# Fused LayerNorm, S5 scan and SwiGLU on one core: one row sum of the fast product made by an accumulating DMA, its seven products reordered

## The chip, the core and the metric

The kernel runs on one core of a Trainium2 chip. The metric is the device time of one execution in microseconds (us); shorter is better. Before the change the median of 7 runs is 204.39 us, from 203.69 to 205.23.

## The reference

The input x has 2048 rows (time steps) of 512 columns. With xn the layer-normalised x, the output is the sum of three things:

```python
xn = layernorm(x)
# S5: a complex diagonal recurrence over time, 512 states, then a projection
h[t] = Lam_bar * h[t-1] + xn[t] @ B_bar.T
ssm  = 2 * Re(h @ C.T) + xn * Dskip
# SwiGLU, inner width 1792
glu  = (silu(xn @ w1) * (xn @ w3)) @ w2
out  = x + ssm + glu
```

All inputs and the output are bf16.

## The kernel before

**Blocks and chunks.** The 2048 rows are worked in four blocks of 512 (b = 0 to 3), each of four chunks of 128 rows. For a block the kernel normalises and transposes xn, makes the gate tiles (`glu`, L519: two matmul groups for each of 14 inner tiles f; ScalarE evacuates both at L534 and L535, VectorE multiplies them at L543), makes the scan's input (`bu`, L425), and runs the scan on VectorE (`ssm_tasks`, L443: products with a cosine and sine table at L457 and L461, an add by an accumulating DMA at L468, scans at L478, products at L484 and L488, an accumulating DMA at L492). Gates and states end as 22 tiles of 128 inner columns, all in one fp16 buffer `act(b)`, of which there are two.

**The fast product.** The output of two chunks (a pair, n = 0 to 7, two for each block) is a product of a matrix A (256 rows by 22 inner tiles) with the stacked weights w2 and C (22 inner tiles by 512 columns). Split in halves both ways, it is a two-by-two product, and the kernel does it in Winograd's form with 7 products in place of 8. Each product (`mms`, L722) is 11 matmuls of 128x256. It needs sums of the blocks of A, and sums of the weights (`weight_sums`, made once). The sums of A are

- S1 = A21 + A22, S3 = A11 - A21, S2 = S1 - A11 (`row_sums`, L676), three VectorE instructions at L683 for each pair. S1 and S2 go to buffers of their own (`homes`), S3 is written over A21;
- S4 = A12 - S2 (L766), written over A12 inside `y_fast`.

**`y_fast(n)`, L708,** issues the seven products of a pair in this order: A11, S1, A12, S2, A22, S4, S3 (for the last pair S3 stands ahead of S4). They accumulate into four PSUM tiles named g, f, z and e; e is seeded by ScalarE at L705 (`seeds`) from the residual. Between the products ScalarE copies g to f and e to an fp32 strip `q[1]` (`copy`, L744), and VectorE adds PSUM tiles to the residual rows (`add`, L735). A finished chunk of 128 rows is stored to HBM by the SyncE queue at L738.

**What sets the order.** The order on each engine is written by the program and is fixed when it is built. Background VectorE work is kept in a list (`Filler`, L24); `fill` releases tasks from it as long as an account of VectorE's time stays within a lead of the account of TensorE's, and `flush(key)` releases all up to a key. Background ScalarE work is in a second list, `sins`; `steps()` in `y_fast` issues two of its entries at a place for block 0. There stand the LayerNorm statistics of blocks 2 and 3 (`ln_scalar_engine`, L262): for each of 4 chunks a sum (L269), then squares (L275), then the normalised row (L285), which ends with a DMA transpose on SyncE's queue (L242). Between these, GpSimd turns sums into a mean (L272) and squares into a reciprocal root (L278, L279, L280). GpSimd also issues the accumulating DMAs, in its program order.

**Around the pairs.** After the gates of block 1 come pairs 0 and 1 (block 0), then the gates of block 2, `bu(3)`, pairs 2 and 3 (block 1), the gates of block 3, and pairs 4 to 7.

Of the kernel before, what the change touches and what calls it, by code (L numbers as in the profile page):

```python
# [11 lines left out]
ALU = mybir.AluOpType  # L12
ACT = mybir.ActivationFunctionType

FP32 = DT.float32
BF16 = DT.bfloat16
FP16 = DT.float16
P = 128
# [45 lines left out]
def kernel(  # L64
# [454 lines left out]
    def glu(b):  # L519
        xnT = xnT_blk[b]  # L520
        pend = []

        def mms(ps, w, f, tsl):
            for dt in range(NDT):
                nc.tensor.matmul(out=ps[:, tsl], lhsT=w[:, dt, f * P:(f + 1) * P], rhs=xnT[:, dt, tsl],  # L525
                                 start=(dt == 0), stop=(dt == NDT - 1))

        pair = []

        def evac(f, g_ps, u_ps):  # L530
            if f % 2 == 0:
                pair[:] = [glup.tile([P, 2, TBLK], BF16, name="g16"), glup.tile([P, 2, TBLK], BF16, name="u16")]
            g16, u16 = pair
            nc.scalar.activation(out=g16[:, f % 2, :], in_=g_ps, func=ACT.Silu)  # L534
            nc.scalar.activation(out=u16[:, f % 2, :], in_=u_ps, func=ACT.Copy)  # L535
            if f % 2 == 1:
                pend.append((f, g16, u16))

        def gate():
            f, g16, u16 = pend.pop(0)  # L540
            bg.own(0.6, -0.5)
            k0, k1 = k_gate(f - 1), k_gate(f)
            nc.vector.tensor_tensor(out=act(b)[:, k0:k1 + 1:k1 - k0, :], in0=g16, in1=u16, op=ALU.mult)  # L543

        f0 = 0
        if b == 0:
            f0 = FIRST
            tiles = first_ps

            def quarter(cl, fs, parts=1):  # L550
                tsl = slice(cl * P, (cl + 1) * P)
                n = NDT // parts
                for side, w in ((0, w1_sb), (1, w3_sb)):
                    for i in range(0, NDT, n):
                        for f in fs:
                            for dt in range(i, i + n):
                                nc.tensor.matmul(out=tiles[2 * f + side][:, tsl], lhsT=w[:, dt, f * P:(f + 1) * P],  # L557
                                                 rhs=xnT[:, dt, tsl], start=(dt == 0), stop=(dt == NDT - 1))

            ln_stats(0, 0)  # L560
            ln_first_rstd(0)
            bulk_loads()
            ln_stats(0, 1)
            ln_first_rstd(1)
            ln_first_transpose(0, 2)
            keep_busy(4, P)
            ln_apply(0, 1)
            ln_first_transpose(1)
            ln_stats(0, 2)
            ln_first_rstd(2)  # L570
            ln_stats(0, 3)
            ln_first_rstd(3)
            ln_apply(0, 2)
            ln_apply(0, 3)
            quarter(0, (0, 1), 2)
            quarter(1, (0, 1))
            pps = params_transpose()
            params_dt(pps)
            params_turn()
            table_angles(0)  # L580
            table_angles(1)
            ln_first_transpose(2)
            quarter(0, (2,))
            ln_first_transpose(3)
            quarter(1, (2,))
            nc.scalar.activation(out=rho, in_=kr, func=ACT.Exp)
            nc.scalar.preload_act_table_set("silu_and_others")
            quarter(2, range(FIRST))
            for f in range(FIRST):
                quarter(3, (f,))  # L590
            evac(0, tiles[0], tiles[1])
            evac(1, tiles[2], tiles[3])
            evac(2, tiles[4], tiles[5])
            gate()
            bg.tensor(0.0)
            bg.fill()
        for f in range(f0, NFT):
            if f == AHEAD[b]:
                if b == 0:
                    ssm_tasks(0)  # L600
                bu(b)
            g_ps = ps_gu.tile([P, TBLK], FP32, name="gu_ps")
            mms(g_ps, w1_sb, f, slice(0, TBLK))
            u_ps = ps_gu.tile([P, TBLK], FP32, name="gu_ps")
            mms(u_ps, w3_sb, f, slice(0, TBLK))
            evac(f, g_ps, u_ps)
            if b in (1, NBLK - 1) and f == NFT - 3:
                seeds(0 if b == 1 else 4)
            if b == 0 and f == FIRST:
                sin_step((0, 0))  # L610
            elif b > 0 or f != MID - 1:
                sin_step()
            bg.tensor(1.72)
            bg.fill()
            if pend and f % 2 == 0:
                gate()
        return gate
# [29 lines left out]
    def weight_sums():  # L647

        def parts(kh, dsl):
            return w2_sb[:, kh * NFH:(kh + 1) * NFH, dsl], weight_state(kh, dsl)  # L650

        def own(i):
            return tw[:, i, 0:NFH, :], tw[:, i, NFH:NK, :]

        def in_place(v):
            return v[0].bitcast(FP16), v[1]

        b11, b12, b21, b22 = parts(0, D1), parts(0, D2), parts(1, D1), parts(1, D2)
        t1, (t2, t3, t4) = in_place(b12), (own(i) for i in range(3))
        def add(i, which):  # L660
            out, x, z = ((t1, b12, b11), (t2, b22, t1), (t3, b22, b12), (t4, b21, t2))[which]
            bg.add((1.1, 0.7)[i], lambda: nc.vector.tensor_tensor(
                out=out[i], in0=x[i], in1=z[i], op=ALU.subtract), "tw")

        return add

    def sum_homes():
        n = NK * P
        spare = tw[:, 3, :, :].rearrange("p k d -> p (k d)")
        xs = [x_blk[i].rearrange("p c d -> p (c d)") for i in range(2)]  # L670
        q = [v[:, n:n + 2 * DH].bitcast(FP32) for v in (*xs, bt.rearrange("p r t d -> p (r t d)"))]
        return [[v[:, 0:n] for v in xs], [spare[:, 0:n], spare[:, n:2 * n]]], q

    sums = {}
# [1 line left out]
    def row_sums(n, b, p):  # L676
# [1 line left out]
        r1, r2 = slice(2 * p * P, (2 * p + 1) * P), slice((2 * p + 1) * P, (2 * p + 2) * P)  # L678
        a11, a12 = a[:, 0:NK, r1], a[:, NK:2 * NK, r1]
        a21, a22 = a[:, 0:NK, r2], a[:, NK:2 * NK, r2]  # L680
        s1, s2 = (v.bitcast(FP16).rearrange("p (k t) -> p k t", t=P) for v in homes[n % 2])
        sums[n] = dict(a11=a11, a12=a12, a22=a22, s1=s1, s2=s2, s3=a21)
        return [(0.9, lambda out=out, x=x, z=z, op=op: nc.vector.tensor_tensor(out=out, in0=x, in1=z, op=op), ("sums", n))  # L683
                for out, x, z, op in ((s1, a21, a22, ALU.add), (a21, a11, a21, ALU.subtract),
                                      (s2, s1, a11, ALU.subtract))]

    seeded = {}

    def seeds(n):
        b, p = pairs[n]  # L690
# [17 lines left out]
    def y_fast(n, then=()):  # L708
# [26 lines left out]
            nc.vector.tensor_tensor(out=out, in0=x, in1=w, op=ALU.add)  # L735

        def store(cl, o, dsl=slice(0, D), eng=nc.sync):
            eng.dma_start(out=ov[:, b * CPB + cl, dsl], in_=o[:, dsl])  # L738

        def right(cols):  # L740
            return slice(DH + cols.start, DH + cols.stop)
# [1 line left out]
        def copy(out, x):  # L743
            nc.scalar.activation(out=out, in_=x, func=ACT.Copy)  # L744
# [5 lines left out]
            add(o2[:, D1], z, q[0])  # L750
            store(c1 + 1, o2)

        q_12 = q[2] if last else q[0]
        mms(g, v["a11"], weight(0, D1), True)
        copy(f, g)
        steps()
        bg.fill()
        for t, cols in halves:
            mms(t, v["s1"], tsum[0], False, cols)
            copy(q[1][:, cols], t)  # L760
            steps()
        bg.first(list(then))
        mms(f, v["a12"], weight(1, D1), False)
        v["s4"] = v["a12"]
        bg.own(0.85, -1.1)
        nc.vector.tensor_tensor(out=v["s4"], in0=v["a12"], in1=v["s2"], op=ALU.subtract)  # L766
        add(o1[:, D1], f, o1[:, D1])
        if n + 1 < len(pairs) and n not in (1, 3):
            seeds(n + 1)
        steps()  # L770
        mms(g, v["s2"], tsum[1], False)
        steps()
        add(q_12, g, o1[:, D2].bitcast(FP16))
        bg.fill()
        mms(z, v["a22"], tsum[3], True)
        steps()
        bg.fill()
        if last:
            store(c1, o1, D1)
            product7()  # L780
        for t, cols in halves:
            mms(t, v["s4"], weight(1, D2), False, cols)
            add(o1[:, right(cols)], t, q_12[:, cols])
            if last:
                store(c1, o1, right(cols), nc.scalar if cols.stop == DH else nc.sync)
        steps()
        if not last:
            store(c1, o1)
            bg.fill(0.5 if n in (1, 3) else None)
            product7()  # L790
            steps()
            bg.fill()

    ln_alloc(0)
    ln1a, ln1b = ln_tasks_vector(1)
# [43 lines left out]
    gate()  # L839
    bg.flush(("sums", 0))  # L840
    bg.first([(0.0 if kept else 0.2, keep_ends, ("ends", 0))])
    y_fast(0, row_sums(1, *pairs[1]))
    ln_scalar_engine(3, lambda cl: ps_y.tile([P, D], FP32, name="y_ps"), sins, (0, 2, 5))
    y_fast(1)
    sin_step(("ln", 2, True))
    res_difference(1)
    ssm_tasks(2, between=row_sums(2, *pairs[2]))
    gate = glu(2)
# [50 lines left out]
```

## Time and profile before

| | |
|---|---|
| the profiled execution's own time | 204.24 us |
| its span, first to last instruction | 202.4 us |
| median of 7 runs (lowest, highest) | 204.39 us (203.69, 205.23) |
| TensorE busy, share of the span | 197.5 us, 98% |
| VectorE busy | 172.5 us, 85% |
| ScalarE busy | 124.9 us, 62% |
| GpSimd busy | 44.2 us, 22% |
| granted TensorE clock | 1.000 |
| DMA on GpSimd's queue | 9.44 MB, 25.0% of 16 engines' span |

Times within the profile are counted from the start of the span. An engine that is busy for 98% of the span by this table may still be served late or early by the others; what it waited for is told by the view of waits, and what ended last by the chain.

### The profile page before, as it was taken

What the parts mean: (1) busy time and instruction counts of PE and PEld (TensorE: products, weight loads), DVE (VectorE), ACT (ScalarE), POOL (GpSimd) and SP (SyncE); (2) the same over time, 40 slices, a digit from 0 to 9 for tenths busy, and PEclk for the clock granted to TensorE, in tenths of its full rate; (3) what the DMA queues carried; (4) which work ended last, traced back from release to release, by engine and by line L of the source; (5) the groups of instructions that cost most, each with busy time, mean ns of one, the idle gap of its engine ahead of it and who ended that gap; (6) DMA issues with size and microseconds to landing.
All of it is one profiled execution on the core that took longest, in us unless ns stands there. A gap on an engine that the chain in (4) does not pass through costs nothing.

```text
span 202.4 us, 3438 instructions
## 1 busy us (share of the span) xinstructions
PE 197.5 (98%) x1304; PEld 123.0 (61%) x1317; DVE 172.5 (85%) x242; ACT 124.9 (62%) x251; POOL 44.2 (22%) x68
## 2 busy tenths in 40 slices
PE   8999999999999999999999999999999999999994
PEld 2874444444444588854444446888444458888993
DVE  4599699999999999989949999999999935584833
ACT  4699797799999966789866676110577662101010
POOL 7170279700310053262111010310101110000000
PEclk9999999999999999999999999999999999999999
DMA  6999995990582043926796014566330880101011
GB/s 170 325 250 228 305 153 160 296 269 3 104 155 56 0 86 72 177 85 107 92 191 129 4 24 83 104 131 133 91 65 0 155 159 1 52 3 52 29 40 39
DMA packets 28816, 23.16 MB, mean 114 GB/s; under 512 B 16128, under 2 KB 26496, under 8 KB 28800
## 3 DMA queue, kind: packets, MB, share of 16 engines
q1 hardware_dynamic: 25536, 13.21, 25.9%
q0 software_dynamic: 2688, 9.44, 25.0%
q10 hardware_dynamic: 576, 0.30, 0.5%
q8 instruction: 10, 0.16, 0.3%
q14 instruction: 6, 0.05, 0.1%
HBM read 7.74 MB, written 2.10 MB: 49 GB/s over the span
## 4 chain that ended last, share of the span: by engine, by line
PE 94%; DMA 2%; SPq 1%; DVE 1%; issue 1%
PE gu_ps L525 45%; PE gu_ps L724 16%; PE y_ps L724 9%; PE bu_ps L724 7%; PE y_ps L435 7%; PE bu_ps L435 7%; DMA w_sb<-in_B_w_dram 2%; PE gu_ps L557 2%; PE bu_ps L557 1%; DVE xn L735 1%; SPq L161 0%; PE y_ps L238 0%; SPq L151 0%; DVE x_blk L735 0%; SPq L163 0%
## 5 line engine op out<-in xcount | busy, mean ns | idle before, releaser
L525 PE MATMUL gu_ps<-xnT,w_sb 128*128 128x512 bf16 x415 | 91.9, 379 | 0.5
L525 PEld LDWEIGHTS <-w_sb 128*128 128x128 bf16 x424 | 41.5, 98 | 49.3
L724 PEld LDWEIGHTS <-act 128*128 128x128 f16 x451 | 43.2, 98 | 5.5
L534 ACT ACTIVATE g<-gu_ps 128x512 bf16<-128x512 f32 x55 | 33.0, 601 | 13.2 <-PE gu_ps L525 12.6
L535 ACT ACTIVATE u<-gu_ps 128x512 bf16<-128x512 f32 x55 | 33.2, 603 | 9.8 <-PE gu_ps L525 9.5
L435 PEld LDWEIGHTS <-bt 128*128 128x128 bf16 x128 | 12.5, 98 | 15.1
L543 DVE TENSOR_TENSOR act<-g,u 128x1024 f16<-128x1024 bf16 x28 | 19.0, 680 | 3.1 <-ACT u L535 3.1
L478 DVE TENSOR_TENSOR_SCAN u<-rho,act,u 128x512 bf16<-128x512 f32 x16 | 19.6, 1270 | 0.0
L492 POOL DMA_DIRECT2D act<-p x8 | 7.1, 885 | 42.3 <-DVE act L488 30.9
L435 PE MATMUL y_ps<-xnT,bt 128*128 128x512 bf16 x63 | 15.1, 379 | 0.1
L435 PE MATMUL bu_ps<-xnT,bt 128*128 128x512 bf16 x61 | 14.8, 379 | 0.1
L457 DVE TENSOR_TENSOR p<-u,tabe 128x2048 bf16<-128x2048 bf16 x8 | 9.8, 1221 | 2.7 <-DMA act<-p 2.6
L468 POOL DMA_DIRECT2D u<-p x6 | 5.2, 875 | 27.5 <-ACT u L535 7.9
L724 PE MATMUL y_ps<-tw,act 128*128 128x256 f16 x88 | 10.9, 273 | 0.0
L724 PE MATMUL gu_ps<-w_sb,act 128*128 128x256 bf16 (+1 forms) x84 | 10.8, 268 | 0.0
L724 PE MATMUL gu_ps<-tw,act 128*128 128x256 f16 x88 | 10.7, 273 | 0.0
L437 ACT ACTIVATE u<-bu_ps 128x512 bf16<-128x512 f32 x16 | 9.4, 597 | 2.0 <-PE bu_ps L435 1.6
L437 ACT ACTIVATE u<-y_ps 128x512 bf16<-128x512 f32 x16 | 9.5, 596 | 1.8 <-PE y_ps L435 1.3
L744 ACT ACTIVATE bu_ps<-y_ps 128x256 f32<-128x256 f32 x4 | 1.5, 368 | 13.7 <-PE y_ps L724 13.7
L461 DVE TENSOR_TENSOR u<-u,tabe 128x2048 bf16<-128x2048 bf16 x8 | 9.8, 1222 | 0.2
L478 DVE TENSOR_TENSOR_SCAN u<-rho,ends,u 128x512 bf16<-128x512 f32 x8 | 9.9, 1272 | 0.0
L484 DVE TENSOR_TENSOR p<-u,tabe 128x2048 f16<-128x2048 bf16 x8 | 9.8, 1224 | 0.1
(146 smaller groups left out, 280.6 us busy)
## 6 DMA issues: line engine op xcount, KB each, us to landing
act<-p POOLq DMA_DIRECT2D x8, 512.0 KB, 4.8
u<-p POOLq DMA_DIRECT2D x6, 512.0 KB, 4.9
xn<-x_blk POOLq DMA_DIRECT2D x4, 512.0 KB, 5.9
out_dram<-xn SPq DMA_DIRECT2D x15, 128.0 KB, 1.7
w_sb<-in_B_w_dram SPq DMA_DIRECT2D x1, 1792.0 KB, 7.8
w_sb<-in_B_w_dram SPq DMA_DIRECT2D x2, 768.0 KB, 5.8
w_sb<-in_B_w_dram SPq DMA_DIRECT2D x4, 256.0 KB, 4.8
w_sb<-in_B_w_dram SPq DMA_DIRECT2D x2, 512.0 KB, 6.1
```

The lines of the kernel that those rows point to most:

```text
L435: nc.tensor.matmul(out=ps, lhsT=bt[:, ri, dt, pt * P:(pt + 1) * P], rhs=xnT_blk[b][:, dt, :], start=(dt == 0), stop=(dt == NDT - 1))
L437: nc.scalar.activation(out=u[:, j, ri, :], in_=ps, func=ACT.Copy)
L457: nc.vector.tensor_tensor(out=st["p"][:, :, ::-1, :], in0=st["g"], in1=tabe[:, psl, 2:0:-1, :], op=ALU.mult)
L461: nc.vector.tensor_tensor(out=st["g"], in0=st["g"], in1=tabe[:, psl, 0:1, :].to_broadcast(FULL), op=ALU.mult)
L478: nc.vector.tensor_tensor_scan(out=v, data0=rho[:, pt:pt + 1].to_broadcast([P, TBLK]), data1=v, initial=init, op0=ALU.mult, op1=ALU.add)
L484: nc.vector.tensor_tensor(out=st["p16"][:, :, ::-1, :], in0=st["g"], in1=tabe[:, psl, 1:3, :], op=ALU.mult)
L492: gp.dma_start(out=act_state(b, hf), in_=st["p16"], accum_op=ALU.add)
L525: nc.tensor.matmul(out=ps[:, tsl], lhsT=w[:, dt, f * P:(f + 1) * P], rhs=xnT[:, dt, tsl], start=(dt == 0), stop=(dt == NDT - 1))
L534: nc.scalar.activation(out=g16[:, f % 2, :], in_=g_ps, func=ACT.Silu)
L535: nc.scalar.activation(out=u16[:, f % 2, :], in_=u_ps, func=ACT.Copy)
L543: nc.vector.tensor_tensor(out=act(b)[:, k0:k1 + 1:k1 - k0, :], in0=g16, in1=u16, op=ALU.mult)
L724: nc.tensor.matmul(out=out, lhsT=left[:, k, :], rhs=right[k][:, cols], start=(start and k == 0), stop=(k == NK - 1), skip_group_check=True)
```

## The change

In `row_sums`, S3 now goes to a buffer of its own and S1 is written over A21. For the pairs of block 0 S1 is still a VectorE add; for pairs 2 to 7 it is a DMA on GpSimd's queue that adds A22 onto A21 in place. S2 is formed as A22 - S3, which is the same sum. In `y_fast` the order of the products becomes A11, A22, A12, S2, S1, S3, S4 for all pairs, the row sums of the next pair are released after the first product and not after the second, and a third strip q[2], a new tile, is used for every pair and not for the last alone. The four stores of block 0 are held and issued after the transposes of block 2 have been issued. In `glu`, the lead of `fill` in the last three inner tiles is smaller for blocks 1 to 3.

```diff
-            bg.fill()
+            bg.fill(-0.7 if b > 0 and f >= NFT - 3 else None)
...
-        q = [v[:, n:n + 2 * DH].bitcast(FP32) for v in (*xs, bt.rearrange("p r t d -> p (r t d)"))]
+        q = [v[:, n:n + 2 * DH].bitcast(FP32) for v in xs]
+        q.append(const.tile([P, DH], FP32, name="q2"))
...
-        s1, s2 = (v.bitcast(FP16).rearrange("p (k t) -> p k t", t=P) for v in homes[n % 2])
-        sums[n] = dict(a11=a11, a12=a12, a22=a22, s1=s1, s2=s2, s3=a21)
-        return [(0.9, lambda out=out, x=x, z=z, op=op: nc.vector.tensor_tensor(out=out, in0=x, in1=z, op=op), ("sums", n))
-                for out, x, z, op in ((s1, a21, a22, ALU.add), (a21, a11, a21, ALU.subtract),
-                                      (s2, s1, a11, ALU.subtract))]
+        s3, s2 = (v.bitcast(FP16).rearrange("p (k t) -> p k t", t=P) for v in homes[n % 2])
+        sums[n] = dict(a11=a11, a12=a12, a22=a22, s1=a21, s2=s2, s3=s3)
+        def subtract(out, x, z):
+            return lambda: nc.vector.tensor_tensor(out=out, in0=x, in1=z, op=ALU.subtract)
+        return [(0.9, subtract(s3, a11, a21), ("sums", n)),
+                (0.9, lambda: nc.vector.tensor_tensor(out=a21, in0=a21, in1=a22, op=ALU.add), ("sums", n)) if b == 0 else
+                (0.0, lambda: gp.dma_start(out=a21, in_=a22, accum_op=ALU.add), ("sums", n)),
+                (0.9, subtract(s2, a22, s3), ("sums", n))]
...
         def store(cl, o, dsl=slice(0, D), eng=nc.sync):
-            eng.dma_start(out=ov[:, b * CPB + cl, dsl], in_=o[:, dsl])
+            if b == 0:
+                held.append((cl, o))
+            else:
+                eng.dma_start(out=ov[:, b * CPB + cl, dsl], in_=o[:, dsl])
```

The body of `y_fast` after the change, whole from the first product on:

```python
        mms(g, v["a11"], weight(0, D1), True)
        copy(f, g)
        bg.first(list(then))
        steps()
        bg.fill(0.8)
        mms(z, v["a22"], tsum[3], True)
        steps()
        bg.fill(0.2)
        mms(f, v["a12"], weight(1, D1), False)
        v["s4"] = v["a12"]
        bg.own(0.85, -1.1)
        nc.vector.tensor_tensor(out=v["s4"], in0=v["a12"], in1=v["s2"], op=ALU.subtract)
        add(o1[:, D1], f, o1[:, D1])
        if last:
            store(c1, o1, D1)
        if n + 1 < len(pairs) and n not in (1, 3):
            seeds(n + 1)
        steps()
        mms(g, v["s2"], tsum[1], False)
        add(q[0], g, o1[:, D2].bitcast(FP16))
        steps()
        bg.fill()
        for t, cols in halves:
            mms(t, v["s1"], tsum[0], False, cols)
            copy(q[1][:, cols], t)
            steps()
        bg.fill(0.5 if n in (1, 3) else None)
        mms(g, v["s3"], tsum[2], False)
        add(q[2], g, o2[:, D1])
        add(o2[:, D2], g, q[1])
        add(o2[:, D1], z, q[2])
        store(c1 + 1, o2)
        for t, cols in halves:
            mms(t, v["s4"], weight(1, D2), False, cols)
            add(o1[:, right(cols)], t, q[0][:, cols])
            if last:
                store(c1, o1, right(cols), nc.scalar if cols.stop == DH else nc.sync)
        if not last:
            store(c1, o1)
        steps()
        bg.fill()
```

After `y_fast(1)` and the last normalisation of block 2:

```diff
     sin_step(("ln", 2, True))
+    for cl, o in held:
+        nc.sync.dma_start(out=ov[:, cl, :], in_=o)
     res_difference(1)
```

More of the change, by code (lines that the diff above doesn't have):

```diff
@@ L680, in row_sums @@
         a21, a22 = a[:, 0:NK, r2], a[:, NK:2 * NK, r2]
-        s1, s2 = (v.bitcast(FP16).rearrange("p (k t) -> p k t", t=P) for v in homes[n % 2])
-        sums[n] = dict(a11=a11, a12=a12, a22=a22, s1=s1, s2=s2, s3=a21)
-        return [(0.9, lambda out=out, x=x, z=z, op=op: nc.vector.tensor_tensor(out=out, in0=x, in1=z, op=op), ("sums", n))
-                for out, x, z, op in ((s1, a21, a22, ALU.add), (a21, a11, a21, ALU.subtract),
-                                      (s2, s1, a11, ALU.subtract))]
+        s3, s2 = (v.bitcast(FP16).rearrange("p (k t) -> p k t", t=P) for v in homes[n % 2])
[6 more added lines that the diff above has]
+                (0.9, subtract(s2, a22, s3), ("sums", n))]
     seeded = {}
+    held = []
     def seeds(n):
@@ L751, in product7 @@
             store(c1 + 1, o2)
-        q_12 = q[2] if last else q[0]
         mms(g, v["a11"], weight(0, D1), True)
         copy(f, g)
+        bg.first(list(then))
+        steps()
+        bg.fill(0.8)
+        mms(z, v["a22"], tsum[3], True)
+        steps()
+        bg.fill(0.2)
+        mms(f, v["a12"], weight(1, D1), False)
+        v["s4"] = v["a12"]
+        bg.own(0.85, -1.1)
+        nc.vector.tensor_tensor(out=v["s4"], in0=v["a12"], in1=v["s2"], op=ALU.subtract)
+        add(o1[:, D1], f, o1[:, D1])
+        if last:
+            store(c1, o1, D1)
+        if n + 1 < len(pairs) and n not in (1, 3):
+            seeds(n + 1)
+        steps()
+        mms(g, v["s2"], tsum[1], False)
+        add(q[0], g, o1[:, D2].bitcast(FP16))
         steps()
@@ L761, in y_fast @@
             steps()
[L762 to L775, printed above, removed]
+        bg.fill(0.5 if n in (1, 3) else None)
+        mms(g, v["s3"], tsum[2], False)
+        add(q[2], g, o2[:, D1])
+        add(o2[:, D2], g, q[1])
+        add(o2[:, D1], z, q[2])
+        store(c1 + 1, o2)
+        for t, cols in halves:
+            mms(t, v["s4"], weight(1, D2), False, cols)
+            add(o1[:, right(cols)], t, q[0][:, cols])
+            if last:
+                store(c1, o1, right(cols), nc.scalar if cols.stop == DH else nc.sync)
+        if not last:
+            store(c1, o1)
         steps()
         bg.fill()
[L778 to L792, printed above, removed]
     ln_alloc(0)
@@ L841 @@
     bg.first([(0.0 if kept else 0.2, keep_ends, ("ends", 0))])
+    bg.flush(("ends", 0))
     y_fast(0, row_sums(1, *pairs[1]))
```

## The prediction

> **What bounds the kernel now.** I read the chain of waits first, then what TensorE waited for, because a change in VectorE's work counts only where TensorE stands still for it.
>
> The chain, from the page (shares of the span by engine; by line it is nearly all L525, L435 and L724, the matmuls):
>
> ```profile
> PE 94%; DMA 2%; SPq 1%; DVE 1%; issue 1%
> ```
>
> The view of waits has two for TensorE's matmuls (us in total, times, longest), and both lie in the first 13 us:
>
> ```profile
> PE bu_ps L191 <- PEq L883: 0.8, 1, 0.8
> PE gu_ps L557 <- DMA w_sb<-in_B_w_dram: 0.4, 1, 0.4
> ```
>
> The timeline of TensorE shows how tightly pairs 0 and 1 are packed (start, us, line, shape):
>
> ```profile
> 69.80 0.93 PE L724 MATMUL y_ps<-w_sb,act 128*128 128x256 bf16 x7
> ...
> 78.20 0.93 PE L724 MATMUL gu_ps<-w_sb,act 128*128 128x256 bf16 x7
> ...
> 86.61 1.24 PE L525 MATMUL gu_ps<-xnT,w_sb 128*128 128x512 bf16 x4
> ```
>
> Pair 0 runs from 69.80 to 78.20 and pair 1 to 86.61: 8.40 each, seven products of 1.20, no gap. Later pairs start at 124.60, 133.0, 165.58, 173.98, 182.39 and 190.80 (the last two from TensorE's rows, the others by steps of 8.40), at the same 8.40. From 13 us to the last matmul near 199.3 TensorE never waits, and the clock granted is 1.000. After that come an add that waits for the last product (199.46, 0.29) and a store, both left as they are. So the change adds no gain wherever it lightens another engine; it can only make TensorE wait. The question is where.
>
> **Removed from VectorE.** Six S1 adds at L683, 0.88 each: 5.3 us less on an engine for which TensorE does not wait. Worth 0. The matmuls keep number and shape: 0. The held stores: in the built order SyncE issues block 2's transposes ahead of those four stores both before and after, so 0. The tile q[2] is only a place. The changed leads of `fill` act only through the order, which is counted below.
>
> **Moved: the products on VectorE.** S2 is added from g into q[0] after the fourth product, and the sixth (S3) now writes g again, one product (1.20) later; before, it was the seventh. In pair 0 the row sums of pair 1 now stand ahead of S4. Taking their steps from the rows (0.92, 0.81, 0.81) from 71.35, when the last gate of block 1 is done (its ScalarE copy ends at 70.60, then 0.60 and a short copy), they end at 73.89; S4 0.80 and two adds 0.34 and 0.33 end at 75.36. The sixth product starts at 69.80 + 5 x 1.20 = 75.80. It fits by 0.4. If VectorE is later than that, each us costs one. After pair 1, block 2's second gate group (0.86 after the end) takes tile e, which is now read last: add 0.2 + 0.42 = 0.62, fits by 0.2. I count 0 for both, at most 0.3 each.
>
> **Moved: the copy of e on ScalarE.** Here I find a wait. The copy to q[1] reads e after the S1 product; the S4 product writes e. Before, S1 was second and S4 sixth; now they are fifth and seventh, one product (1.20) apart. ScalarE works in order, and in the built order of block 0's pair 0 its queue reads: square, copy of g, three squares, seed, one normalisation (L285), copy of e. That L285 waits for GpSimd's three steps on the squares. The timelines of ScalarE and GpSimd before:
>
> ```profile
> 72.90 0.36 ACT L744 ACTIVATE x_blk<-bu_ps 128x256 f32<-128x256 f32 x1
> 73.17 0.71 ACT L275 ACTIVATE xn<-x_blk,acc 128x512 bf16<-128x512 bf16 x1
> 73.78 0.19 ACT L275 ACTIVATION_READ_ACCUMULATOR xn<-x_blk,acc 128x1 f32 x1
> ...
> 76.90 2.93 ACT L285 ACTIVATE xn<-x_blk,acc,rstd_all 128x512 bf16<-128x512 bf16 x4 [2.65 <-POOL acc L280]
> ```
>
> ```profile
> 74.07 0.46 POOL L278 TENSOR_SCALAR acc<-acc 128x4 f32<-128x4 f32 x1 [0.76 <-ACT xn L275]
> 74.61 1.64 POOL L279 TENSOR_TENSOR rstd_all<-acc,mhalf 128x4 f32<-128x4 f32 x1
> 76.33 0.54 POOL L280 TENSOR_TENSOR acc<-acc,rstd_all 128x4 f32<-128x4 f32 x1
> ```
>
> The copy of e stood at 72.90, ahead of the wait of 2.65; it now stands behind it. The fourth square takes its place at 72.90, its read-out ends 0.80 later, at 73.70; GpSimd starts 0.10 later, at 73.80, and ScalarE follows 2.83 after that start (74.07 to 76.90 in the rows): 76.63. One L285 steps 0.71 ((2.93 - 0.81)/3, with 0.81 the median of one): the copy starts at 77.34, takes 0.36 and ends at 77.70. The S4 product could start at 69.80 + 6 x 1.20 = 77.00. TensorE waits **0.7**. Bounds: the same three steps took 3.64 at 87.90 to 91.54, which makes it 1.5; a chain of 2.1 or less makes it 0, and no row is that short. I take 0.7, the chain in the same place. The other three normalisations follow the copy and end near 79.9, against 79.83 before, so block 2's transposes, issued from them, stay in time.
>
> Pair 1 then starts at 78.90. There the copy of e stands behind four sums (L269), a GpSimd step (L272) and two squares. Copy of g 1.43 after the start (1.40 in pair 0, 1.46 in pair 2), 80.33; sums from 80.6 for 2.55, to 83.15; L272 took 0.46 once and 1.23 once, so 83.7 to 84.5; two squares 1.4, the copy 0.36: 85.5 to 86.3. Needed at 78.90 + 7.20 = 86.10. That is 0 to 0.2; I take **0.1**. The pairs of other blocks have no such work in ScalarE's queue: 0.
>
> **Added: S1 by DMA.** Six transfers of 128 x 11 pieces of 256 bytes, 352 KB. The nearest rows are the accumulating DMAs of 512 KB in 128 pieces of 4 KB, and the tiny ones of 4 pieces, in the answers on lines L492 and L200 (issue on GpSimd in ns, least/median/most; then landing in us):
>
> ```profile
> L492 POOL DMA_DIRECT2D act<-p x8: 853/860/985, 38.4 to 162.0; - x8
> ...
> DMA to landing us min/median/max: 4.6/4.8/8.1
> ```
>
> ```profile
> L200 POOL DMA_DIRECT2D par_rows<-in_A_Lambda_im_dram x1: 498/498/498, 2.8 to 2.8; - x1
> ```
>
> Low end: 4.8, as for more bytes in fewer pieces (the issue 0.86 of it). High end: issue in proportion to the pieces, 11 x 0.86 = 9.5, and the other 3.9 behind it: 13.4. Between 4 and 128 pieces the issue grows by (860 - 498)/124 = 2.9 ns a piece, which gives 0.86 + 1280 x 2.9 ns = 4.6, and with 3.9 a landing of 8.5. I take 8.5, since it rests on two rows and not on one.
>
> The time there is: S1 is the fifth product, 4.80 after its pair starts. Pair 2: made long ahead, in block 2's gates. Pair 3: S3 ends near 128.2 (behind the same VectorE work that ends at 127.3 before), needed at 137.8: 9.6. Pair 4: made before block 3's gates, idle. Pair 5: S3 follows the gate of 166.41 and ends near 167.9, needed at 178.8: 10.9. Pairs 6 and 7: S3 follows the last add of two pairs before the product, near 175.4 and 183.8, needed at 187.2 and 195.6: 11.8 each. At 8.5 all fit: **0**. On GpSimd's queue each S1 stands ahead of other transfers, above all pair 4's ahead of block 3's first scan add (L468): 4.6 of issue delays it to about 141, landing near 146; scans start then and not at 143.8. VectorE's gates may be late by some 4 us before ScalarE's three gate buffers run out, so 0.
>
> A rule speaks against these pieces. The Trainium skill, DMA: Bandwidth & Descriptors, section Specifications, asks for transfers of at least 512 bytes for line rate; no row here has an accumulate with pieces that small. The same page's fit (Anatomy of one DMA, SWDGE path), 2.0 us plus bytes over 436 GB/s, gives an estimate of 3.2 for 512 KB, where the trace has 4.8, and 2.8 for S1, by which the sum would also have 0.
>
> **Sum.** 204.24 (span 202.4 and 1.84 around it) + 0.7 + 0.1 = 205.04. The median stands 0.15 above the profiled execution, so I forecast 205.2. About 0.3% (0.6 us) is what a measurement of this kernel can tell from no change.
>
> **Rivals.** (1) *Not slower.* ScalarE's copy comes in time: if GpSimd's chain ends before 75.9 the wait is gone, and 204.3 remains. For it: GpSimd no longer issues a scan add just before the chain (the L468 row at 72.42). Against it: the chain waited for ScalarE then, not for that issue. Chance 0.26, with the cases where the wait comes out half as long.
> (2) *S1 lands late.* At 13.4, pair 3 waits 3.8, pair 5 2.5, pair 6 nothing (pair 5's wait gives it time), pair 7 1.6: 7.9 more, 213. It decides from 9.6 on; at 11 it is 1.4 + 0.1, which gives 206.7. For it: no row has pieces this small. Against: the slope between two rows. Chance 0.24.
> (3) *Faster.* It would need TensorE waits that this execution does not show, or a shorter end; runs reach down to 203.7. Chance 0.08.
> The forecast itself has 0.42.
>
> **Numbers.** The forecast's own range is 204.9 to 206.0 (chain 2.83 to 3.64, pair 1 0 to 0.2). Faster 0.08; same 0.26; slower 0.42 + 0.24 = 0.66. The range 204.0 to 208.5 leaves out the lower part of (3) and the later half of (2), under 0.2.
>
> **What would show it.** Right: in the waits, TensorE waits about 0.7 for ScalarE's L755 in pair 0, none on DMAs; the S1 issue on GpSimd is 3 to 5 us; the last product is moved by the sum of these. Wrong: TensorE waits on the S1 transfer (then (2)), on VectorE's adds (my 0.4 was too thin), or not at all (then (1)).

## The result and the profile after

The changed kernel takes 205.09 us (median of 24 runs, 204.55 to 207.22) against 203.97 for the kernel before (59 runs in the same comparison): a ratio of 1.0056, 95% interval 1.0043 to 1.007. It is slower by 0.6%, or 1.1 us; the forecast was 205.2. The profiled execution took 204.66 us with a span of 202.6. Ratios and intervals leave out slow executions, over 1.5% above the fastest of the same kernel, while medians and ranges are of all runs unless the text says otherwise.

The chain now has ScalarE and GpSimd in it, where before it had SyncE and a load (in the rerun e0 below it has all four):

```profile
PE 93%; ACT 2%; POOL 1%; issue 1%; DVE 1%
```

The waits of TensorE's matmuls (us in total, times, longest) hold the wait at start-up and a new one. The wait of 0.4 for weights is not there in this execution; in the rerun e0 it is, with 0.2.

```profile
PE bu_ps L191 <- PEq L898: 0.8, 1, 0.8
PE bu_ps L732 <- ACT x_blk L755: 0.6, 1, 0.6
```

Where it is, the timeline of TensorE tells: between pair 0's sixth product and its seventh, S4. The third row is block 2's first gate group.

```profile
75.25 1.36 PE L732 MATMUL y_ps<-tw,x_blk 128*128 128x256 f16 x11
77.20 0.93 PE L732 MATMUL bu_ps<-w_sb,act 128*128 128x256 bf16 x7 [0.59 <-ACT x_blk L755]
...
86.80 5.56 PE L525 MATMUL gu_ps<-xnT,w_sb 128*128 128x512 bf16 x24
```

From start to start it is 1.95 where a product takes 1.20, so 0.75 is lost. Pair 0 began at 69.24 here and at 69.80 before; between runs this start moves by 0.5 or more. I therefore compare executions by the *middle*, from the start of pair 0 to block 2's first gate group: 16.81 before, 17.56 after, 0.75 more. From there to the end of the span both take 115.8. So all that this span shows of the change lies in pair 0. The timelines of ScalarE and GpSimd show why:

```profile
72.97 0.19 ACT L275 ACTIVATION_READ_ACCUMULATOR xn<-x_blk,acc 128x1 f32 x1
...
76.06 0.82 ACT L285 ACTIVATE xn<-x_blk,acc,rstd_all 128x512 bf16<-128x512 bf16 x1 [2.63 <-POOL acc L280]
76.78 0.36 ACT L755 ACTIVATE x_blk<-bu_ps 128x256 f32<-128x256 f32 x1
```

```profile
73.24 0.20 POOL L278 TENSOR_SCALAR acc<-acc 128x4 f32<-128x4 f32 x1 [5.27 <-ACT xn L275]
73.52 1.56 POOL L279 TENSOR_TENSOR rstd_all<-acc,mhalf 128x4 f32<-128x4 f32 x1
75.16 0.87 POOL L280 TENSOR_TENSOR acc<-acc,rstd_all 128x4 f32<-128x4 f32 x1
77.53 0.93 POOL L468 DMA_DIRECT2D u<-p  x1 [1.50 <-DVE u L461]
```

The copy of e (L755) stands behind one normalisation (L285), which waits for GpSimd's three steps. The last row matters later: the first half of block 1's scan add, issued at 72.42 before, is now issued at 77.53, because VectorE's products for it (L457, L461) come later.

S1's six transfers, from the answer on their line:

```profile
L691 POOL DMA_DIRECT2D act<-act x6: 1908/1928/2244, 110.1 to 184.3; - x6
...
DMA to landing us min/median/max: 6.6/7.1/7.9
```

Issue takes 1.93 and landing 7.1; no engine's wait is put down to them.

### The profile page after: what moved, and what is told of

Read it like the earlier page. It is cut to its first block, busy times and chain, and to the rows that moved or that the text cites. A ratio compares the mean times of both kernels' runs of the same rounds, so it can differ in the third digit from the quotient of the medians.

```text
span 202.6 us, 3435 instructions
## 1 busy us (share of the span) xinstructions
PE 197.6 (98%) x1304; PEld 123.0 (61%) x1317; DVE 168.6 (83%) x236; ACT 125.4 (62%) x251; POOL 53.6 (26%) x74
## 3 DMA queue, kind: packets, MB, share of 16 engines
q0 software_dynamic: 11232, 11.60, 39.6%
## 4 chain that ended last, share of the span: by engine, by line
PE 93%; ACT 2%; POOL 1%; issue 1%; DVE 1%
PE gu_ps L525 45%; PE gu_ps L732 16%; PE y_ps L732 7%; PE y_ps L435 7%; PE bu_ps L435 7%; PE bu_ps L732 6%; PE bu_ps L191 2%; PE gu_ps L557 2%; ACT xn L275 1%; PE bu_ps L557 1%; POOL rstd_all L279 1%; PE y_ps L238 1%; DVE xn L743 1%; POOL acc L280 0%; ACT u L535 0%
## 5 line engine op out<-in xcount | busy, mean ns | idle before, releaser
L492 POOL DMA_DIRECT2D act<-p x8 | 7.1, 893 | 42.8 <-DVE act L488 31.2
L691 POOL DMA_DIRECT2D act<-act x6 | 11.9, 1991 | 17.1 <-DVE tw L687 8.9
L732 PE MATMUL gu_ps<-w_sb,act 128*128 128x256 bf16 (+3 forms) x112 | 14.1, 266 | 0.0
L732 PE MATMUL bu_ps<-w_sb,act 128*128 128x256 bf16 (+3 forms) x98 | 12.2, 265 | 0.6 <-ACT x_blk L755 0.6
L457 DVE TENSOR_TENSOR p<-u,tabe 128x2048 bf16<-128x2048 bf16 x8 | 9.8, 1220 | 2.2 <-DMA act<-p 2.0
L461 DVE TENSOR_TENSOR u<-u,tabe 128x2048 bf16<-128x2048 bf16 x8 | 9.8, 1224 | 0.2
L488 DVE TENSOR_TENSOR act<-u,tabe 128x2048 f16<-128x2048 bf16 x8 | 9.8, 1220 | 0.0
L775 DVE TENSOR_TENSOR act<-act,tw 128x1408 f16<-128x1408 f16 x4 | 3.6, 892 | 7.0 <-PE gu_ps L732 5.4
```

The costliest lines, as they stand in the source:

```text
L457: nc.vector.tensor_tensor(out=st["p"][:, :, ::-1, :], in0=st["g"], in1=tabe[:, psl, 2:0:-1, :], op=ALU.mult)
L461: nc.vector.tensor_tensor(out=st["g"], in0=st["g"], in1=tabe[:, psl, 0:1, :].to_broadcast(FULL), op=ALU.mult)
L691: (0.0, lambda: gp.dma_start(out=a21, in_=a22, accum_op=ALU.add), ("sums", n)),
L732: nc.tensor.matmul(out=out, lhsT=left[:, k, :], rhs=right[k][:, cols], start=(start and k == 0), stop=(k == NK - 1), skip_group_check=True)
```

## The experiments

Medians and ratios are against the kernel before on the same chip. The labels of the theories are those of each expectation alone.

**Four kernels on one chip (before: 204.04).** First the changed kernel again, unaltered.

> The changed kernel unaltered, beside the others on one chip. Theory A (the wait of TensorE for ScalarE's copy of e in pair 0 is the whole cost, 0.75 us from start to start in its profile): ratio 1.004, so 0.7 to 0.9 us above the kernel before. Theory B (the wait and something more, of the DMA or of the end of the program): 1.0056 again, 1.0 to 1.3 us.

Measured: 205.1, ratio 1.0041 (1.0025 to 1.0056). The five executions of the ratio have a median of 204.97; the other three took 209.72, 210.26 and 213.22, with a mean granted clock of 0.992, 0.992 and 0.983, and of the 13 executions of the kernel before beside them none is above 204.93. In the profile the wait for L755 is there again, 0.6, and the middle is again 17.56.

Then the copy put ahead of the first normalisation. The third number says how late ScalarE's list releases L285:

```diff
-    ln_scalar_engine(2, lambda cl: xn_blk[2][:, cl, :], sins, (0, 1, 4))
+    ln_scalar_engine(2, lambda cl: xn_blk[2][:, cl, :], sins, (0, 1, 5))
```

> Only the order of two instructions of ScalarE in pair 0 differs from the changed kernel: the copy of e stands ahead of the first normalisation of block 2, so it no longer waits for GpSimd's chain. Theory A: the wait of 0.75 is gone, nothing takes its place, and the time is that of the kernel before, ratio 1.000 within 0.002. Theory B: 0.3 to 0.4 us stay, ratio 1.0015 to 1.002. Rival C (the wait was only the first in line, and VectorE's add into q[0] or the tile e is late next): 0.2 to 0.6 us stay, and the waits name VectorE.

Measured: 206.66, ratio 1.0131 (1.01 to 1.0162). It is slower than the changed kernel by 1.5, and no theory had expected that. The wait for the copy has gone; in TensorE's waits another stands in its place:

```profile
PE gu_ps L525 <- DMA xnT<-xn: 2.3, 1, 2.3
```

Block 2's gates now wait for its DMA transposes. From the answer on the transposes' line (issue on SyncE's queue, then landing):

```profile
L242 SPq DMA_TRANSPOSE xnT<-xn x4: 1217/1691/2287, 77.4 to 83.3; - x4
...
DMA to landing us min/median/max: 3.4/4.7/5.6
```

The last is issued at 83.3, takes 5.6, and lands at 88.9; the gates could have begun at 86.5, one pair's 8.41 after 78.11. In the changed kernel the last was issued at 82.6 and landed near 85.8, against gates at 86.80. GpSimd's two scan adds of 512 KB (L468) are issued at 77.99 and 82.90 here, so one lies beside the first transposes and the other is issued ahead of the last. In the changed kernel the second was issued at 83.18, behind the last transpose. Without the wait in pair 0, VectorE's work that follows TensorE comes 0.75 earlier, and with it this transfer: 13.19 after the start of pair 0, where it was 13.94.

The kernel before shows the same within one execution. Its second scan add was issued at 80.30. Of its four transposes the two issued ahead of that, at 77.7 and 79.1, landed in 2.4 each; the two behind it took twice that, and the last landed at 86.4, 0.2 ahead of the gates at 86.61:

```profile
L242 SPq DMA_TRANSPOSE xnT<-xn x2: 1219/1915/2611, 80.4 to 81.7; - x2
...
DMA to landing us min/median/max: 4.7/5.2/5.7
```

That reading asked for a kernel in which the scan adds are out of the way, which is f1 below.

The third and fourth kernels give S1 back to VectorE for all pairs, with the copy where the change has it and with the copy first:

```diff
-                (0.9, lambda: ... out=a21, in0=a21, in1=a22, op=ALU.add), ("sums", n)) if b == 0 else
+                (0.9, lambda: ... out=a21, in0=a21, in1=a22, op=ALU.add), ("sums", n)) if b >= 0 else
```

> S1 of every pair is an add on VectorE again, in place on A21; the order of the products and the wait in pair 0 stay. Theory A: the wait of 0.75 stays, the DMA was worth nothing either way, ratio as the changed kernel run beside it, within 0.002. Theory B with the DMA as its cause: 0.3 to 0.4 us less than the changed kernel. Rival D (the DMA does relieve VectorE where it counts): slower than the changed kernel by 0.3 us or more, with TensorE waiting for VectorE's sums or adds.

> The copy of e ahead of the normalisation, and S1 on VectorE in every pair: what is left of the change is the order of the products, S2 as A22 less S3, the third strip and the held stores. Theory A: ratio 1.000 within 0.002, as with the copy moved alone. Theory B with the DMA as its cause: 0.3 to 0.4 us below the kernel with the copy moved alone. Rival D: above that kernel by 0.3 us or more.

Measured: 206.46 (1.0128, 1.0093 to 1.0163) and 208.13 (1.0203, 1.0178 to 1.0228). That is 1.4 and 1.5 more than with S1 by DMA (205.1 and 206.66). The second has e1's wait for the transposes too (2.2). Beside that, TensorE's waits have a new row, and VectorE's waits a row on L690, the S1 add:

```profile
PE gu_ps L732 <- DVE x_blk L743: 1.0, 1, 1.0
```

```profile
DVE act L690 <- DMA act<-p: 2.5, 1, 2.5
```

The S1 add waits on VectorE for a transfer of the scan, and the adds behind it come late to TensorE. As a DMA, S1 waits on GpSimd's queue and nothing else of VectorE's stands behind it. The transfer itself is later, too: the scan's last (L492) is issued at 176.8 here and at 167.1 in e1, since with S1 on VectorE the list places the scan's last products behind pair 5's sums. So within this order the DMA is worth 1.4 to 1.5 us; the runs don't separate the 0.88 of each add from the order that comes with it.

The profile of e2 is of its longest execution, 210.77, and says nothing of the 1.4. But it shows that e1's second wait can come while the first is there. TensorE waits 0.6 for the copy in pair 0 and then for the transposes, of which the slowest took 6.2 (5.2 in the changed kernel's profile), and the clock granted after that is half (stretch, us, busy, granted clock, DMA share, GB/s):

```profile
PE gu_ps L525 <- DMA xnT<-xn: 2.1, 1, 2.1
```

```profile
90.00:92.00 2.00, 2.00 (x5) 0.50 0.35 120
92.00:94.00 2.00, 2.00 (x8) 0.68 0.00 0
```

**Four more on another chip (before: 204.12).** Two order effects undone together: the copy first, as above, and the smaller lead of `fill` left off for block 1, which puts the scan's products and the first scan add back ahead.

```diff
-            bg.fill(-0.7 if b > 0 and f >= NFT - 3 else None)
+            bg.fill(-0.7 if b > 1 and f >= NFT - 3 else None)
...
-    ln_scalar_engine(2, lambda cl: xn_blk[2][:, cl, :], sins, (0, 1, 4))
+    ln_scalar_engine(2, lambda cl: xn_blk[2][:, cl, :], sins, (0, 1, 5))
```

> Two of the order effects undone in the changed kernel, nothing else. The smaller lead of `fill` at the end of the gates is left off for block 1, which puts block 1's first half of products (L457, L461) and its accumulating DMA (L468) back ahead of pair 0's S4 difference, as before; and the copy of e (L755) stands ahead of the first normalisation L285 on ScalarE. Theory A (the change lost its time by two order effects around block 2's transposes, the copy behind the normalisation and the scan's accumulating DMA moved into the transposes; S1 by DMA and the products' new order cost nothing): no wait of TensorE for ScalarE's copy, the transposes' landings back to at most 4.7 us apart from one, no wait or at most 0.3 us before block 2's gates, and the time of the kernel before, 204.0, within 0.4. Theory B (something else in the change, as the S1 DMA or VectorE's order in pairs 2 to 7, holds 0.4 us or more): 204.5 to 205. Rival C (taking the copy's wait away uncovers the transposes whatever the accumulating DMAs do): a wait of 1 to 2.3 us before block 2's gates remains, 205.5 to 206.5.

Measured: 204.52, ratio 1.0019 (1.0006 to 1.0033). Both waits are gone. The transposes, issued no earlier than in e1, land in half the time:

```profile
L242 SPq DMA_TRANSPOSE xnT<-xn x4: 1211/1218/1625, 78.0 to 82.3; - x4
...
DMA to landing us min/median/max: 2.4/2.5/2.7
```

GpSimd issued the first scan add at 72.66 and the second at 83.48, behind the issue of the last transpose (82.3), so that at most their ends meet. Between e1 and this kernel only block 1's lead differs, and that is worth 2.2 us (2.6 above the kernel before there, 0.4 here). The middle is 17.03, still 0.22 above before; TensorE's timeline shows where:

```profile
75.64 0.60 PE L732 MATMUL bu_ps<-ct,act 128*128 128x256 f16 x4
76.30 1.36 PE L732 MATMUL y_ps<-tw,x_blk 128*128 128x256 f16 x11
```

From start to start 0.66, where 0.44 is usual: the S3 product waits for VectorE's add out of g, which ended at 76.24, since VectorE now has the scan's products ahead of S4.

The lead alone, with the copy left behind the normalisation:

> The smaller lead of `fill` left off for block 1 alone; the copy of e stays behind the first normalisation. Theory A: the wait for the copy stays, 0.6 to 1.0 us (GpSimd now issues the scan's accumulating DMA ahead of its chain L278 to L280, as before, so the chain may end 0.3 later), the transposes are not disturbed: 204.0 + 0.75 = 204.8, from 204.6 to 205.1. Theory E (the 0.3 to 0.4 us by which the medians differ more than the profile's 0.75 would give come from executions in which block 2's transposes land late beside the moved accumulating DMAs): then this kernel is faster than the changed one by 0.3. Rival: the accumulating DMAs matter only when the copy's wait is away, then this kernel has the changed kernel's time, 205.1.

Measured: 205.08 (1.0046, 1.0029 to 1.0063), the changed kernel's time. Its transposes land in 2.4 to 4.0 (what slowed the 4.0, with no scan add issued between 72.04 and 83.63, is open), and its wait for the copy is 0.6. In the medians, then, the disturbed transposes cost nothing while the wait for the copy is there, as the rival had it. In single executions they can, as e2's profile shows, and the times of the changed kernel spread further: of its 32 runs (24, and 8 in e0) seven lie above 205.8, while of the 32 of f1, f2 and g1, which all put the first scan add back, none is above 205.49. None of the seven has a profile.

The changed kernel with a longer chain on GpSimd, by doubling the power instruction:

```diff
+                if b == 2:
+                    gp.tensor_tensor(out=rstd, in0=ss, in1=mhalf, op=ALU.pow)
```

> The changed kernel with GpSimd's power instruction (L279) issued twice for block 2, the same result written again: a chain longer by one such instruction, 1.6 us in the profile of the changed kernel. Theory A (TensorE's wait in pair 0 is for the copy, which stands behind a normalisation that waits for this chain): the wait grows one for one, from 0.6 to 2.2 us, and since the transposes and the gates that need them move together, nothing more is added: 205.1 + 1.6 = 206.7. Rival (the wait comes from the seven products' order or from the copy's own time): no change, 205.1.

Measured: 206.35 (1.0108, 1.0091 to 1.0125). In TensorE's waits (the lines are moved by two):

```profile
PE bu_ps L734 <- ACT x_blk L757: 1.8, 1, 1.8
```

The chain, from the start of L278 to the end of its last step, is 4.05 and was 2.79. It grew by 1.26 and not by 1.6, since its last step came out shorter (0.37, not 0.87). The middle grew by 1.26 too (18.82 against 17.56), and the median by 1.2 (2.23 above the kernel before on its chip, 1.06 in e0): one for one.

The changed kernel with block 0's stores issued where they are made:

```diff
-            if b == 0:
-                held.append((cl, o))
-            else:
-                eng.dma_start(out=ov[:, b * CPB + cl, dsl], in_=o[:, dsl])
+            eng.dma_start(out=ov[:, b * CPB + cl, dsl], in_=o[:, dsl])
```

> The changed kernel with block 0's four stores issued where `y_fast` makes them and not held. In this order of products two of them stand ahead of block 2's transposes on SyncE's queue, and the second waits for pair 0's last adds (79.0 us in the changed kernel's trace), with about 1 us for each store's issue: the four transposes, 1.7 us each, then start near 81 in place of 76.9, the last is issued near 86 and lands near 89 to 91, against gates that want it at 86.8. Theory A (the transposes' issue and landing decide when block 2 begins, and have about 1 us to spare): a wait of 2 to 4 us before block 2's gates, 207 to 209. Rival (the gates' wait does not follow the queue, the prediction's term of 0 holds without the hold too): 205.1.

Measured: 209.78 (1.0265, 1.0231 to 1.0298), above the range given. SyncE's timeline and the wait:

```profile
77.41 5.65 SPq L242 DMA_TRANSPOSE xnT<-xn  x3
83.17 1.00 SPq L747 DMA_DIRECT2D out_dram<-xn  x2
84.26 1.51 SPq L242 DMA_TRANSPOSE xnT<-xn  x1
```

```profile
PE gu_ps L525 <- DMA xnT<-xn: 2.9, 1, 2.9
```

The stores stand ahead of the last transpose only, not of all four. Counted from pair 0's start, that transpose is issued 1.1 later than in the changed kernel (14.5 against 13.4), and so behind the second scan add (83.69); it takes 6.1 to land, where it took 3.2. TensorE stands for 3.1 us (87.31 to 90.37). What I had not priced is the clock after that. The windows of TensorE (stretch, us, busy, granted clock, DMA share, GB/s) show it at half:

```profile
90.00:92.00 2.00, 1.41 (x3) 0.50 0.14 49
92.00:94.00 2.00, 2.00 (x8) 0.68 0.00 0
```

From block 2's gates to the end this kernel takes 117.2, 1.4 more than the usual 115.8. The sum is 0.75 + 3.06 + 1.4 = 5.2, and the span is 5.2 longer than before.

**Two more (before: 204.24).** f1 with one instruction moved in pair 0, the S4 difference behind the two adds:

```diff
-        nc.vector.tensor_tensor(out=v["s4"], in0=v["a12"], in1=v["s2"], op=ALU.subtract)
+        if n > 0:
+            difference()
...
         add(q[0], g, o1[:, D2].bitcast(FP16))
+        if n == 0:
+            difference()
```

> The kernel of f1_lead_and_copy with one VectorE instruction moved: in pair 0 the S4 difference (L775, 0.88 us) stands behind the first two adds and not ahead of them. In f1's trace VectorE comes late to pair 0 (block 1's products L457 and L461 stand ahead of it), the add that frees g for the S3 product ends at 76.2, and TensorE loses 0.22 us between the S1 and the S3 product. Theory A (that 0.22 is all that is left inside the span; the other 0.15 or so by which f1 is slower lies outside it, between the span and the whole time, 1.95 us against 1.83): the wait goes, S4 is done 0.2 us ahead of its product, and the time is 204.1 + 0.15 = 204.25, from 204.0 to 204.5. Rival (the difference is now late instead): the same 204.5 or more.

Measured: 204.0, ratio 0.9997 (0.9984 to 1.0009): the time of the kernel before. In TensorE's timeline pair 0's steps are regular, and the middle is 86.14 - 69.33 = 16.81, as before:

```profile
75.33 1.36 PE L732 MATMUL y_ps<-tw,x_blk 128*128 128x256 f16 x11
76.53 0.93 PE L732 MATMUL bu_ps<-w_sb,act 128*128 128x256 bf16 x7
...
86.14 2.11 PE L525 MATMUL gu_ps<-xnT,w_sb 128*128 128x512 bf16 x9
```

So with three orders set right, the whole rest of the change (S1 by DMA, the new product order, the held stores, and a flush of one short copy ahead of pair 0 that the list of the change leaves out) costs nothing and gains nothing that this comparison can tell.

Last, the DMA without the new order of products: the kernel before, with the new `row_sums` (its diff stands in the change) and nothing else.

> The kernel before with the new `row_sums` alone: S1 by DMA over A21 for pairs 2 to 7, S3 to its own buffer, S2 as A22 less S3; the products keep their order, S1 second. Theory A (S1's DMA costs nothing in the changed kernel because the new order, S1 fifth and the row sums released one product earlier, gives it the time): issued behind the S3 instruction (131.9, 171.8, 180.2 and 188.6 us in the trace of before for pairs 3, 5, 6 and 7) and landing 7.1 us later, as the changed kernel's six did, it comes 4.8 us after the time of pair 3's S1 product (134.2) and 3.7 us after those of pairs 5, 6 and 7; pairs 2 and 4 stand behind gates and have time. 4.8 + 3 x 3.7 = 15.9: 220 us, from 215 to 223. Rival (the landing is short when nothing else moves, or the order was not needed): 204 to 207.

Measured: 229.71, from 227.12 to 231.13, ratio 1.1263 (1.122 to 1.1306): above the range given. The profile is of the shortest run. TensorE waits four times for S1's transfer:

```profile
PE bu_ps L729 <- DMA act<-act: 9.4, 2, 5.5
PE gu_ps L729 <- DMA act<-act: 7.6, 2, 3.9
```

In the timeline they are 5.47, 3.75, 3.88 and 3.85, in sum 16.95 where I had worked out 15.9. The rest is the clock again: after three of the four waits it is granted at 0.50, and TensorE's busy time is 203.4 in place of 197.5. 16.95 + 5.9 is the 22.9 by which the span is longer. The new order, with S1 fifth and the sums released a product earlier, is therefore what makes room for the DMA; the two parts were not tried apart.

## Why the prediction held, and where it did not

**The time: 205.2, measured 205.09, and so near by luck.** The forecast added 0.8 to a median of 204.39; 1.1 were measured, on 203.97. A base 0.4 too high and a difference 0.3 too low nearly cancel. The forecast's own range, 204.9 to 206.0, was counted without the 0.15 that 205.2 has; with it, it is 205.1 to 206.1.

**The wait in pair 0: 0.7, measured 0.75.** The mechanism is shown from both sides: with the copy ahead of the normalisation the wait goes (e1, f1, g1), and with a longer chain it grows one for one (f3). The chain took 2.79, I took 2.83. The chain's length is not fixed, though: in the same place it took 3.02 in f1 and 2.28 in g1, and with 2.28 the same sum gives a wait of 0.15.

**Pair 1: 0.1, measured 0.** It lasted 8.41. The copy of e ended 6.6 after the pair's start (85.00), the low end of what was worked out, and was needed after 7.2.

**S1 by DMA: 0, measured 0, by terms that were too large.** The issue is 1.93 and not 4.6 (of the signs named, "3 to 5 us" did not come), the landing 7.1 and not 8.5. The slope of 2.9 ns a piece between a transfer of 4 pieces and one of 128 did not carry on: from 128 to 1408 pieces it is (1928 - 860)/1280 = 0.8. The room of 9.6 to 11.8 was enough, and g2 shows what it is worth. The fit that the prediction weighed (the Trainium skill, DMA: Bandwidth & Descriptors, section Anatomy of one DMA, SWDGE path) gave an estimate of 2.8 for S1; the trace has 7.1, and the measurement decides.

**VectorE's margin before the sixth product: 0.4, measured 0.42** (the add ended at 74.83, the product began at 75.25). That it counted, f1 shows, where the same margin is overdrawn by 0.22.

**The six adds "worth 0": true against the kernel before, not within the new order.** There an S1 on VectorE costs 1.4 to 1.5 (e2, e3), through the transfer that it waits for.

**The held stores: 0 against before; in the new order the hold is worth some 4.7** (209.78 - 205.1, on two chips). I compared the queue of before with that of after and did not ask what the queue would be without the hold.

**What the prediction left out is the landing of the transposes.** "Block 2's transposes, issued from them, stay in time" was worked out to ScalarE's normalisations, not to the landing. In the changed kernel's profile it held by about 1 us, with landings of up to 5.2; in e2's execution it did not hold, and in e1, without the first wait, it failed by 2.3. The prediction had named that GpSimd no longer issues a scan add ahead of the chain, for rival (1), and did not follow where it went: into the transposes. Rival (1) itself, a shorter chain, was not tried. A shorter chain would also bring the transposes forward; e1 changes only the order and takes 206.66, not the 204.3 of that rival, and f1, with the scan add back in its place, takes 204.52.

**What stays open.** The medians of before and after differ by 1.1, the spans' middles by 0.75. About 0.1 lies around the span: time less span has a median of 1.93 to 2.01 in the kernels with the new order that were compared above, and of 1.81 to 1.84 before; g2, which keeps the old order, has 1.84. Which part of the new order does that wasn't tried. Some 0.2 is left in the comparison of 24 runs, near what medians of this kernel move from chip to chip (203.97 to 204.24 for the kernel before); in e0 the five executions of the ratio are 0.93 above the kernel before, and 0.75 and 0.15 fill that. The upper runs of the changed kernel, to 207.22 and in e0 to 213.22, have no profile; that they are late transposes, as in e2's, is likely and not shown.

## What to carry to other kernels

When products are reordered, go through every in-order queue that serves them, and look for a short instruction that now stands behind a long wait; here a 0.36 us copy behind a chain of 2.8 cost the whole 0.75. Before you price "and if that wait isn't there", work out the next deadline behind it, to the landing of its transfers and beside what they run: here the fix of the first wait alone cost another 1.5 us. This sum took longer by DMA than on the engine (7.1 against 0.88), so it needed an order that uses it later; even then it gained nothing over the kernel before.

## What the runs showed of the hardware

- A DMA transpose beside accumulating DMAs of 512 KB landed in 3.4 to 5.6 us, and in 2.4 to 2.7 without them (e1, f1); in one execution of the kernel before, in 2.4 ahead of such a DMA and in 4.7 and 5.7 behind its issue.
- Accumulating pieces of 256 bytes were dear for the DMA engines. GpSimd's queue had 25.0% of 16 engines' span before and 39.6% after, for 8,544 more packets and 2.16 MB: 474 us of engine time, 56 ns a packet, 4.6 bytes a ns, where the 9.44 MB before went at 11.7. This agrees with the rule of 512 bytes in the Trainium skill, DMA: Bandwidth & Descriptors, section Specifications, though no run here tries a size between. In the new order it cost TensorE nothing.
- After TensorE stood still for 2.1 (e2), 2.9 (f4), 3.85, 3.88 and 5.5 us (g2) the granted clock was 0.50 for the next 2 to 4 us; after 1.8 (f3), 2.2 (e3) and 2.3 us (e1), and once after 3.75 (g2), it stayed at 1.00. The Trainium skill, TensorE: Matmul & The Clock Gate, section Why this matters for your kernels, warns of gaps over about 3 us. These runs agree only in part: 2.1 was enough once, and 3.75 was not, so the length of the gap alone did not decide. A wait of 2 us or more has to be priced with slow matmuls that may follow it: 1.4 us in f4, 5.9 in g2.
